# Weight signs by a parametric ReLU, 128-row values, long weight rows and filling products from the start, in an attention and channel-mix kernel

## The chip, the cores and the metric

The kernel runs on one core of one Trainium2 chip. The core has five engines that work side by side, each through its own instructions in order: TensorE (PE in the profile, its weight loads PEld), VectorE (DVE), ScalarE (ACT), GpSimd (POOL) and SyncE (SP), which here issues every DMA. The metric is the device time of one execution in microseconds; lower is better.

## The reference

Two blocks follow each other: attention with a local window and block summaries, and a gated channel mix over the concatenated heads.

```python
# attention: B, H, S, D = 4, 8, 768, 64; block 32, window 16
k_sum = k.reshape(B, H, nb, block, D).max(axis=3)
v_sum = v.reshape(B, H, nb, block, D).mean(axis=3)
scores_l = scale * q @ k^T, masked to |i - j| < 16
scores_s = scale * q @ k_sum^T + log(block)
a = softmax(concatenate([scores_l, scores_s]))
attn = a @ concatenate([v, v_sum])
# channel mix: x = attn as (4, 768, 512); d_ff = 1024
x_prev = x shifted by one token
xk = mu_k * x + (1 - mu_k) * x_prev
xr = mu_r * x + (1 - mu_r) * x_prev
k = maximum(xk @ w_k, 0)
out = sigmoid(xr @ w_r) * ((k * k) @ w_v)
```

The weights arrive in double precision, everything else in single.

## The kernel before

**Tiling.** The tokens of each of the four batches are cut into two halves of 384 (hf 0 and 1), the heads into four pairs p. A *unit* is one pair of one half: its scores (L466, 24 passes into sc), mask and row minimum on VectorE (L477), exponentials with row sums on ScalarE (L481), inverse sums (L487, L488), normalisation on GpSimd (L493), transposes on TensorE (L500), their copy to SBUF (L504), the product with the values (L513, into av) and the copy of the result (vx, L524 or L526). Each score tile has 120 columns: 64 + 32 keys of the window and 24 block maxima, which VectorE makes of the keys (L381 to L393). The values stand in vx with 120 rows to match; the block means are a product with the small table pool_sb (L405), a copy, a selection (L425) and a copy into the 24 middle rows (L431).

**Mix, gate, experts.** L535 or L538 and L541 mix a half's result with its shifted self. For the very first half (batch 0, hf 0) gate and experts work in plain float32: L580 multiplies the mixes of pair p with w_r (12 products into three PSUM tiles), L558 takes the sigmoid of each tile into z, L601 is xk @ w_k (one j of eight, 128 columns of w_k), L608 and L610 are ReLU and square, L627 the product with w_v. For the seven other halves each operand is split into a high and a low part, and each product is three (L567 to L569 for the gate, L601 and L627 again for the experts).

**Weights.** They are sent as 64-bit words. A weight step loads 128 rows of 4096 bytes into one of three buffers st (L310; w_k comes as four runs of 1024 bytes in each row), then builds float32 of the two words: ScalarE (L318) or GpSimd (L321) scales the upper word, read as a float, into wc; VectorE shifts three bits out of the lower word into the single buffer we (L325), puts the sign of the upper word beside them (L328), and joins both (L332). There are 20 steps: four of w_r, eight of w_k and eight of w_v in turn. Later L349 or L350 (high part) and L352 (low part) split each.

**Order.** Nothing is issued as written. All operations are recorded with an expected length (table LENGTH), a due time and the buffers they take, and a planner (`schedule`) plays the engines through: at each step it takes for each engine the operation that can start first or is due first, and gives buffers in turn. An operation with two ways, like L318 and L321, goes to the engine that would end it first. Loads are played as one queue with a fixed time and so many bytes a nanosecond. The engines then run the instructions in the planned order, waiting where reality is later. Up to 150 filling products (`warm`, L680: identity by identity, once the identity has landed) may be placed where TensorE has nothing due, until the last of the float32 gate is planned.

Of the kernel before, what the change touches and what calls it, by code (L numbers as in the profile page):

```python
# [18 lines left out]
DM, DF = 512, 1024  # L19
# [24 lines left out]
    exp=380, pts=380, vm=160, mixa=520, cast=405, relu=525, square=530, sigmoid=500, wscale=570, wcast=530,  # L44
# [4 lines left out]
DMA_NS_PER_BYTE = 1 / 290.0  # L49
# [8 lines left out]
WARM = 150  # L58
COLD = 10000
# [39 lines left out]
class Plan:  # L99
# [36 lines left out]
    def schedule(self):  # L136
# [27 lines left out]
        spare = [o for o in self.ops if o.name == "warm"]  # L164
        while any(ready.values()):
            best = None
            for e, now in engines.items():
# [53 lines left out]
            if o.name == "gate32" and spare:  # L221

                for w in spare:
                    for x in w.bufs:
                        x.left -= 1
                        if not x.left:
                            free_slots[x.pool].append((start, x.place))
                spare = []
                ready["PE"] = [x for x in ready["PE"] if x[0].name != "warm"]
            if o.name == "warm":  # L230
                spare.remove(o)
# [8 lines left out]
def tile_kernel(ctx: ExitStack, tc: tile.TileContext, q, k, vT, v, mask, ident, pool, sel, mu, w_k, w_v, w_r, out):  # L240
# [36 lines left out]
    MASK, IDENT, MU, OM, POOLM, SEL = [((x, 0),) for x in ("mask", "ident", "mu", "om", "pool", "sel")]  # L277
# [23 lines left out]
    def weight(name, i, src, last, due=None):  # L301
        st, we, wc = buf("st"), buf("we"), buf("wc")
        wf = w_f[name, i] = buf("wc") if last else buf("w", F32, False)
        shape = src.shape
        whole = [(wc, 0)]

        def load():
            s = src.bitcast(U32)
            d = st.t.rearrange("p (c a) -> p c a", c=shape[1]) if len(shape) == 3 else st.t
            nc.sync.dma_start(out=d, in_=s)  # L310

        def words():
            w = st.t.rearrange("p (a b) -> p a b", b=2)
            return w[:, :, 1], w[:, :, 0]


        def scale_act():
            nc.scalar.activation(wc.t.bitcast(F32), words()[0].bitcast(F32), AF.Copy, scale=2.0**-112)  # L318
# [256 lines left out]
    def gate_parts(x, z):  # L575
# [7 lines left out]
        for t in range(NTT):  # L583
            sigmoid(ps[t], z[t])
# [218 lines left out]
```

## Time and profile before

| | |
|---|---|
| Time, median of three runs (lowest to highest) | 474.1 us (472.27 to 476.43) |
| The profiled execution's own time | 475.29 us |
| Its span, first to last instruction | 473.5 us |
| TensorE busy | 447.6 us (95%) |
| ScalarE busy | 292.6 us (62%) |
| VectorE busy | 267.0 us (56%) |
| GpSimd busy | 112.5 us (24%) |
| Mean granted TensorE clock | 0.993 of full speed |
| Moved by DMA | 51.16 MB, mean 108 GB/s |

Busy time is time in which an engine's instruction ran; for TensorE the ends of pipelined products are modelled. Times in the trace count from the first instruction. A row of the timeline or of the chain gives the start, the length, engine, line and tiles; "x24" is the number of instructions merged in it, and for TensorE one float32 product is two instructions (passes). What stands in brackets is the time the engine was idle before and what ended it. "issue" is time in which the profile shows nothing to wait for.

### The profile page before, as it was taken

To read this page: it belongs to the slowest core of one execution; us is meant where nothing else is said; L and a number is where in the kernel's file an instruction comes from. 1 tells how busy PE (TensorE), PEld (TensorE's weight loads), DVE (VectorE), ACT (ScalarE), POOL (GpSimd) and SP (SyncE) were. 2 spreads that over 40 slices of the span, in tenths; PEclk is the share of its full clock that TensorE was granted. 3 is DMA by queue.
4 is the path that set the end of the run, shared out by engine and by line. 5 is a ranking of instruction groups with operands and counts; after the bars stand their busy time and mean duration, and the time that the engine had idled before them with its cause. 6 is when DMAs were issued, how large, how long until landed. Compare 5 with 4: busy or idle time off the path is not lost.

```text
span 473.5 us, 9475 instructions
## 1 busy us (share of the span) xinstructions
PE 447.6 (95%) x3438; PEld 357.9 (76%) x3438; DVE 267.0 (56%) x865; ACT 292.6 (62%) x815; POOL 112.5 (24%) x236
## 2 busy tenths in 40 slices
PE   2798799989899999999999999999999999999996
PEld 2664455546688888997778888997778889888995
DVE  3599789989453566527554565529354554222223
ACT  3578987878785756418886756428886655231311
POOL 0453470734133201302442201304242201000000
PEclk9999889999999999999999999999999999999999
DMA  7995368986110209807200219707100010001001
GB/s 245 257 261 158 105 207 262 289 263 148 51 59 12 68 1 304 211 0 228 60 8 9 78 37 301 212 1 219 35 9 9 12 43 26 1 0 68 0 1 66
DMA packets 27013, 51.16 MB, mean 108 GB/s; under 512 B 2903, under 2 KB 14807, under 8 KB 26967
## 3 DMA queue, kind: packets, MB, share of 16 engines
q1 hardware_dynamic: 26967, 50.56, 36.7%
q8 instruction: 27, 0.44, 0.4%
q14 instruction: 19, 0.16, 0.1%
HBM read 42.49 MB, written 6.29 MB: 103 GB/s over the span
## 4 chain that ended last, share of the span: by engine, by line
PE 67%; ACT 12%; DVE 8%; DMA 8%; issue 2%; POOL 1%; SPq 1%; ACTq 0%; POOLq 0%; DVEq 0%
PE mm L627 23%; PE mm L601 22%; ACT y L481 5%; PE pt L500 4%; PE av L513 4%; DMA kt<-in_k 3%; PE mm L567 3%; PE mm L569 3%; PE mm L568 3%; PE sc L466 2%; DMA pool_sb<-in_pool 2%; PE mm L580 2%; ACT L481 2%; DMA st<-in_w_k 1%; POOL y L493 1%
## 5 line engine op out<-in xcount | busy, mean ns | idle before, releaser
L601 PE MATMUL mm<-xs,w 128*128 128x384 f32 x736 | 152.1, 355 | 0.6 <-DVE w L332 0.6
L601 PEld LDWEIGHTS mm<-xs,w 128*128 128x128 f32 x736 | 131.3, 190 | 13.9 <-issue 3.7
L493 POOL TENSOR_SCALAR y<-y,rc 128x120 f32<-128x120 f32 x192 | 93.9, 507 | 156.1 <-DVE rc L488 131.6
L627 PE MATMUL mm<-w,kh 128*128 128x512 f32 x336 | 91.9, 402 | 0.0
L608 ACT ACTIVATE r<-mm 128x384 f32<-128x384 f32 x64 | 31.2, 488 | 93.9 <-PE mm L601 93.8
L481 ACT ACTIVATE y<-y,mn 128x120 f32<-128x120 f32 x192 | 73.5, 386 | 10.7 <-DVE mn L477 10.4
L627 PEld LDWEIGHTS mm<-w,kh 128*128 128x128 f32 x336 | 60.7, 188 | 11.1 <-DVE kl L616 0.2
L614 DVE CAST kh<-r 128x384 fp32r<-128x384 f32 x44 | 15.9, 362 | 74.9 <-ACT r L610 74.8
L477 DVE CUSTOM_DVE_ANT_0 y<-sc,mask_sb 128x120 f32<-128x120 f32 x192 | 42.5, 277 | 22.9 <-PE sc L466 19.6
L627 PE MATMUL mm<-w,kl 128*128 128x512 f32 x168 | 52.4, 407 | 0.1
L549 DVE TENSOR_TENSOR xs<-xa,xs 128x384 fp32r<-128x384 f32 x56 | 30.4, 558 | 23.6 <-ACT xs L547 23.2
L500 PE MATMUL pt<-ident_sb,y 128*120 128x128 f32 x192 | 33.9, 285 | 6.4 <-POOL y L493 6.0
L504 ACT COPY pts<-pt 120x384 f32<-120x384 f32 x64 | 30.3, 473 | 15.6 <-PE pt L500 15.4
L466 PE MATMUL sc<-kt,qt 64*64 64x120 f32 x768 | 30.4, 289 | 8.6 <-DMA pool_sb<-in_pool 6.8
L500 PEld LDWEIGHTS pt<-ident_sb,y 128*120 128x120 f32 x192 | 22.8, 139 | 19.0 <-POOL y L493 9.6
L481 ACT ACTIVATION_READ_ACCUMULATOR y<-y,mn 128x1 f32 x192 | 36.3, 189 | 0.0
L541 DVE SCALAR_TENSOR_TENSOR xa<-vx,mu_sb,xa 128x384 f32<-128x384 f32 x56 | 33.8, 630 | 2.7 <-ACT xa L535 1.8
L627 PEld LDWEIGHTS mm<-w,kl 128*128 128x128 f32 x168 | 30.0, 188 | 6.5 <-DVE kl L616 0.5
L466 PEld LDWEIGHTS sc<-kt,qt 64*64 64x64 f32 x768 | 22.2, 143 | 16.7 <-DVE kt L393 6.8
L567 PE MATMUL mm<-w,xs 128*128 128x512 f32 x84 | 33.6, 400 | 1.1 <-ACT r L608 0.8
L610 ACT ACTIVATE r<-r 128x384 f32<-128x384 f32 x64 | 33.6, 525 | 1.2
L616 DVE TENSOR_TENSOR kl<-r,kh 128x384 fp32r<-128x384 f32 x56 | 31.7, 566 | 4.3 <-ACT kh L615 1.3
(64 smaller groups left out, 548.1 us busy)
## 6 DMA issues: line engine op xcount, KB each, us to landing
vx<-in_v SPq DMA_DIRECT2D x32, 360.0 KB
kt<-in_k SPq DMA_DIRECT2D x15, 544.0 KB
qt<-in_q SPq DMA_DIRECT2D x32, 192.0 KB
out<-z SPq DMA_DIRECT2D x24, 256.0 KB
st<-in_vT SPq DMA_DIRECT2D x12, 384.0 KB
st<-in_w_k SPq DMA_DIRECT2D x8, 512.0 KB
st<-in_w_v SPq DMA_DIRECT2D x8, 512.0 KB
st<-in_w_r SPq DMA_DIRECT2D x4, 512.0 KB
```

The lines of the kernel that those rows point to most:

```text
L466: nc.tensor.matmul(sc[h].t[cs, i, 0:NK], qt.t[hs, n * QW:(n + 1) * QW], kt.t[hs, w * KB:w * KB + NK], start=True, stop=True,)
L477: op("DVE", "mask", None, lambda h=h, i=i, var=var: nc.vector.tensor_tensor_reduce(out=y[h].t[:, i, :], in0=sc[h].t[:, i, 0:NK], in1=mask_ ...
L481: op("ACT", "exp", None, lambda h=h, i=i: nc.scalar.activation(y[h].t[:, i, :], y[h].t[:, i, :], AF.Exp, bias=mn[h].t[:, i:i + 1], scale=-1.0,
L493: op("POOL", "norm", None, lambda h=h, i=i: nc.gpsimd.tensor_scalar(out=y[h].t[:, i, :], in0=y[h].t[:, i, :], scalar1=rc.t[:, NSL * h + i: ...
L500: nc.tensor.transpose(out=pt[h].t[0:NK, i * P:(i + 1) * P], in_=y[h].t[:, i, :], identity=ident_sb)
L541: op("DVE", "mixd", None, lambda: nc.vector.scalar_tensor_tensor(out=xa.t, in0=xt.t[:, 1 + lo:1 + lo + HT], scalar=mu_sb[:, which, p:p + 1 ...
L567: nc.tensor.matmul(ps.t, xh.t[:, ts], h, start=(p == 0), stop=False)
L601: nc.tensor.matmul(ps.t[:, 0:HT], w.t[:, p * P:(p + 1) * P], (x[p] if single else x[p][s]).t, start=(n == 0), stop=(n == len(terms) * NPAI ...
L608: op("ACT", "relu", None, lambda: nc.scalar.activation(r.t, ps.t[:, 0:HT], AF.Relu), reads=[(ps, 0)], writes=[(r, 0)])
L610: op("ACT", "square", None, lambda: nc.scalar.activation(r.t, r.t, AF.Square), reads=[(r, 0)], writes=[(r, 0)])
L616: op("DVE", "sub", None, lambda: nc.vector.tensor_tensor(out=kl.t, in0=r.t, in1=kh.t.bitcast(F32), op=ALU.subtract), reads=[(r, 0), (kh, 0 ...
L627: nc.tensor.matmul(acc[t].t, a.t[:, t * P:(t + 1) * P], v.bitcast(F32) if single else v, start=start, stop=stop)
```

## The change

1. **Weight step.** The scaling on ScalarE becomes a parametric ReLU whose slope for negative inputs, -2^32, leaves the sign where the following shift puts it. VectorE's step for the sign (L328) and GpSimd's way (L321) go. So st is read last by L307 (ScalarE) and L310 (VectorE), lines of the new kernel.
2. **Loads.** w_k is laid out beforehand so that each row of a step is one run of 4096 bytes; the values are padded from 120 to 128 rows (384 KB a load in place of 360).
3. **Filling products** multiply a tile of zeros that GpSimd sets at the start, write the unused end of the transposes' PSUM tile (so they hold no mm tile), and may be placed up to 110 us of the plan wherever TensorE would else be idle for over 0.3 us.
4. **Sigmoids** of the first half are one operation of the plan, so they stand side by side.
5. The planner is told other numbers: 330 bytes a nanosecond for loads in place of 290, and 4.0 us for the three sigmoids.

```diff
-DMA_NS_PER_BYTE = 1 / 290.0
+DMA_NS_PER_BYTE = 1 / 330.0
-WARM = 150
-COLD = 10000
+WARM = 260
+WARM_END = 110000
+GAP = 300
+COLD = 5000
...
+                if e == "PE" and now > WARM_END:
+                    ready[e] = [x for x in ready[e] if x[0].name != "warm"]
                 for o, at in ready[e]:
+                    if o.name == "warm":
+                        fill = max(now, at), o
+                        continue
...
+                if fill and (pick is None or pick[2] > fill[0] + GAP):
+                    pick = None, fill[1], fill[0]
...
-        def scale_act():
-            nc.scalar.activation(wc.t.bitcast(F32), words()[0].bitcast(F32), AF.Copy, scale=2.0**-112)
...
-        def sign():
-            nc.vector.scalar_tensor_tensor(
-                out=we.t, in0=words()[0], scalar=0x80000000, in1=we.t, op0=ALU.bitwise_and, op1=ALU.bitwise_or)
...
+        op("ACT", "wscale", None, lambda: nc.scalar.activation(
+            wc.t.bitcast(F32), words(1).bitcast(F32), AF.Prelu, scale=2.0**-112, alpha=-2.0**32),
+           reads=[(st, 0)], writes=[(wc, 0)])
...
-                out=windows(vw[hf]), in_=v[b, p, hf]),
-               writes=[(vw[hf], "a"), (vw[hf], "b")], size=NK * HW * 512)
+                out=vw[hf].t[:, 0:S], in_=v[b, p, hf]),
+               writes=[(vw[hf], "a"), (vw[hf], "b")], size=P * HW * 512)
...
-        for t in range(NTT):
-            sigmoid(ps[t], z[t])
+        def sigmoids():
+            for t in range(NTT):
+                nc.scalar.activation(z[t].t, ps[t].t, AF.Sigmoid)
+        op("ACT", "sigmoid3", None, sigmoids, reads=[(a, 0) for a in ps], writes=[(a, 0) for a in z])
...
-    spare = buf("mm", F32, False)
+    op("POOL", "tiny", -1.0e6, lambda: nc.gpsimd.memset(zero_sb, 0.0), writes=ZERO)
+    spare = pools["pt"][0][:, 512 - P:512]
     for _ in range(WARM):
         op("PE", "warm", 1.0e8, lambda: nc.tensor.matmul(
-            spare.t[:, 0:P], ident_sb, ident_sb, start=True, stop=True), reads=IDENT, writes=[(spare, 0)])
+            spare, zero_sb, zero_sb, start=True, stop=True), reads=ZERO)
...
-        "w_k": words(inputs["moe_w_k"]),
+        "w_k": words(np.asarray(inputs["moe_w_k"]).reshape(NCK, P, NCV, P).transpose(2, 1, 0, 3), NCV),
```

The planned order on TensorE at the program's start, before (sc: scores of the first and second unit; then pooling and the first transposes; rows left out repeat their neighbours):

```order
L466 MATMUL sc_128<-kt_61,qt_64 64x120 x2
L466 MATMUL sc_129<-kt_61,qt_64 64x120 x2
...
L466 MATMUL sc_128<-kt_62,qt_65 64x120 x2
L466 MATMUL sc_129<-kt_62,qt_65 64x120 x2
...
L405 MATMUL mm_132<-vx_68,pool_sb 32x128 x2
...
L500 MATMUL pt_130<-ident_sb,y_91 120x128 x3
```

and after, with the same names:

```order
L660 MATMUL pt_130<-zero_sb 128x128 x13
L441 MATMUL sc_128<-kt_61,qt_64 64x120 x2
L441 MATMUL sc_129<-kt_61,qt_64 64x120 x2
...
L660 MATMUL pt_130<-zero_sb 128x128 x13
L441 MATMUL sc_128<-kt_62,qt_65 64x120 x2
...
L660 MATMUL pt_130<-zero_sb 128x128 x5
L380 MATMUL mm_132<-vx_68,pool_sb 32x128 x2
...
L475 MATMUL pt_130<-ident_sb,y_91 120x128 x3
```

31 filling products stand before the first pooling where none stood; between there and the last values of the first half are 12 more where 15 were.

TensorE again, from the end of the first half's last values (L513, L488 after) to the transposes of the next unit, before:

```order
L513 MATMUL av_131<-pts_106,vx_77 64x64
L466 MATMUL sc_128<-kt_61,qt_64 64x120 x2
...
L580 MATMUL mm_135<-w_0_524,xs_0_561 128x512
L580 MATMUL mm_133<-w_0_524,xs_0_561 128x512
L580 MATMUL mm_134<-w_0_524,xs_0_561 128x512
L601 MATMUL mm_132<-xs_0_565,w_0_563 128x384
...
L466 MATMUL sc_128<-kt_62,qt_65 64x120 x2
...
L500 MATMUL pt_130<-ident_sb,y_91 120x128 x3
```

and after (xs_0_527 is the third pair's mix, xs_0_578 the fourth's):

```order
L488 MATMUL av_131<-pts_106,vx_77 64x64
L555 MATMUL mm_135<-w_0_513,xs_0_527 128x512
L555 MATMUL mm_132<-w_0_513,xs_0_527 128x512
L441 MATMUL sc_128<-kt_61,qt_64 64x120 x2
...
L660 MATMUL pt_130<-zero_sb 128x128
L555 MATMUL mm_133<-w_0_546,xs_0_578 128x512
...
L441 MATMUL sc_128<-kt_62,qt_65 64x120 x2
...
L660 MATMUL pt_130<-zero_sb 128x128 x5
L475 MATMUL pt_130<-ident_sb,y_91 120x128 x3
L660 MATMUL pt_130<-zero_sb 128x128 x2
```

Two gate products of the third pair now follow the last values, and eight filling products have come in.

ScalarE in the same place, before (wc: a weight step; z: a sigmoid; y: exponentials of the next unit; r: ReLU and square of the first expert):

```order
L318 ACTIVATE wc_126<-st_122 128x512
L349 CAST w_0_581<-w_0_563 128x512
L558 ACT_TABLE_LOAD
L558 ACTIVATE z_108<-mm_135 128x512
L481 ACT_TABLE_LOAD
L481 ACTIVATE y_91,sm_100<-y_91,mn_95 128x120 x3
L481 ACTIVATE y_92,sm_100<-y_92,mn_96 128x120 x3
L558 ACT_TABLE_LOAD
L558 ACTIVATE z_109<-mm_133 128x512
L558 ACTIVATE z_110<-mm_134 128x512
L318 ACTIVATE wc_127<-st_123 128x512
L608 ACTIVATE r_116<-mm_132 128x384
```

and after:

```order
L307 ACTIVATE wc_126<-st_122 128x512
L456 ACTIVATE y_91,sm_100<-y_91,mn_95 128x120 x3
L456 ACTIVATE y_92,sm_100<-y_92,mn_96 128x120 x3
L561 ACT_TABLE_LOAD
L561 ACTIVATE z_108<-mm_133 128x512
L561 ACTIVATE z_109<-mm_135 128x512
L561 ACTIVATE z_110<-mm_132 128x512
L587 ACTIVATE r_116<-mm_134 128x384
L479 COPY pts_107<-pt_130 120x384
L589 ACTIVATE r_116<-r_116 128x384
L307 ACTIVATE wc_127<-st_123 128x512
```

The exponentials of the next unit now stand ahead of the sigmoids, and the first sigmoid's own pair of table loads is gone.

More of the change, by code (lines that the diff above doesn't have):

```diff
@@ L163, in schedule @@
                 released(o)
-        spare = [o for o in self.ops if o.name == "warm"]
         while any(ready.values()):
@@ L220, in schedule @@
             order.append(o)
[L221 to L231, printed above, removed]
             for s in o.succ:
@@ L276, in tile_kernel @@
     sel_sb = const.tile([P, NS], F32, name="sel_sb")
-    MASK, IDENT, MU, OM, POOLM, SEL = [((x, 0),) for x in ("mask", "ident", "mu", "om", "pool", "sel")]
+    zero_sb = const.tile([P, P], F32, name="zero_sb")
+    MASK, IDENT, MU, OM, POOLM, SEL, ZERO = [((x, 0),) for x in ("mask", "ident", "mu", "om", "pool", "sel", "zero")]
     op("SP", "load", None, lambda: nc.sync.dma_start(out=mask_sb, in_=mask), writes=MASK, size=P * 3 * NK * 4)
@@ L331, in join @@
-        def join():
-            nc.vector.scalar_tensor_tensor(
-                out=wf.t.bitcast(U32), in0=wc.t, scalar=3, in1=we.t, op0=ALU.logical_shift_left, op1=ALU.bitwise_or)
-        op("SP", "load", due, load, writes=[(st, 0)], size=P * 4096)
-        op("ACT", "wscale", None, scale_act, reads=[(st, 0)], writes=whole, other=("POOL", "wscale_p", scale_pool))
-        op("DVE", "wbits", None, low, reads=[(st, 0)], writes=[(we, 0)])
-        op("DVE", "wor", None, sign, reads=[(st, 0), (we, 0)], writes=[(we, 0)])
@@ L339, in weight, with words @@
-        op("DVE", "wor", None, join, reads=[(we, 0), *whole], writes=[(wf, 0)])
+        def words(n):
+            return st.t.rearrange("p (a b) -> p a b", b=2)[:, :, n]
+        op("SP", "load", due, lambda: nc.sync.dma_start(out=st.t, in_=src.bitcast(U32)), writes=[(st, 0)], size=P * 4096)
+        op("ACT", "wscale", None, lambda: nc.scalar.activation(
+            wc.t.bitcast(F32), words(1).bitcast(F32), AF.Prelu, scale=2.0**-112, alpha=-2.0**32),
+           reads=[(st, 0)], writes=[(wc, 0)])
@@ L672, in tile_kernel @@
     for i in range(NCK):
-        weight("wr", i, w_r[i * P:(i + 1) * P, :], False)
+        weight("wr", i, w_r[i], False)
     for j in range(NCV):
-        weight("wk", j, w_k[:, j * P:(j + 1) * P].rearrange("(c p) n -> p c n", p=P), False)
-        weight("wv", j, w_v[j * P:(j + 1) * P, :], j == NCV - 1)
-    spare = buf("mm", F32, False)
+        weight("wk", j, w_k[j], False)
+        weight("wv", j, w_v[j], j == NCV - 1)
+    op("POOL", "tiny", -1.0e6, lambda: nc.gpsimd.memset(zero_sb, 0.0), writes=ZERO)
+    spare = pools["pt"][0][:, 512 - P:512]
     for _ in range(WARM):
-        op("PE", "warm", 1.0e8, lambda: nc.tensor.matmul(
-            spare.t[:, 0:P], ident_sb, ident_sb, start=True, stop=True), reads=IDENT, writes=[(spare, 0)])
+        op("PE", "warm", 1.0e8, lambda: nc.tensor.matmul(spare, zero_sb, zero_sb, start=True, stop=True), reads=ZERO)
     sets, gates = [], []
```

35 lines of the change are left out of this document (13 added, 22 removed).

## The prediction

> **What bounds the kernel now.** I read the windows first, cut where the work changes, then the chain of waits of the first 64 us, then the timeline of TensorE where the windows show holes, then the groups by line. Rows of the windows give the stretch, its length, and busy time (with the count of instructions) of PE, PEld, DVE, ACT and POOL, then the granted clock, the DMA share and GB/s:
>
> ```profile
> 16.00:43.00 27.00, 27.00 (x320) 17.89 (x320) 22.21 (x63) 18.38 (x55) 14.55 (x23) 1.00 0.82 220
> 43.00:62.00 19.00, 14.10 (x85) 7.75 (x78) 13.84 (x53) 18.82 (x51) 5.31 (x9) 0.82 0.47 145
> 62.00:109.00 47.00, 44.50 (x311) 24.79 (x309) 44.63 (x128) 37.13 (x107) 21.32 (x37) 1.00 0.87 258
> 109.00:126.00 17.00, 14.66 (x126) 11.01 (x127) 12.14 (x40) 14.10 (x37) 7.25 (x14) 1.00 0.31 78
> 126.00:474.00 348.00, 342.37 (x2539) 292.93 (x2537) 167.19 (x545) 198.46 (x546) 61.45 (x140) 1.00 0.24 72
> ```
>
> The last row settles where a gain can come from: from 126 us to the end TensorE is busy for 342.4 of 348.0 us. The order of its products is the same there in both programs but for a few transposes near the start, so that stretch keeps its length, and the change is worth what it lets that stretch start earlier. Before it, TensorE has no hole from 16 to 43 us, but part of what it does there is filler and part runs slowly; from 43 to 62 us it stands still for 4.9 us and is granted 0.82 of its clock; from 62 to 126 us it stands still for 2.5 + 2.3 = 4.8 us. VectorE is busy for 44.6 of the 47 us after 62 us, so it is next.
>
> The chain of waits up to 64 us, start, length and what (the first line shares the 64 us out):
>
> ```profile
> by line: DMA pool_sb<-in_pool 13.3%; PE mm L580 13.0%; ACT y L481 9.0%; PE mm L680 7.1%; PE pt L500 6.3%; PE mm L405 6.1%; PE av L513 5.3%; ACT L558 4.0%; ACT L481 4.0%; ACT wc L318 3.9%; PE sc L466 3.4%; ACT xs L535 3.4%; SPq L371 3.1%; is
> 6.07 8.51 DMA pool_sb<-in_pool
> 14.63 1.51 PE mm L405 x24
> 16.13 0.83 PE pt L500 x3
> 16.96 1.41 PE sc L466 x24
> 18.37 0.55 PE mm L425 x2
> 18.92 0.83 PE pt L500 x3
> 19.75 1.70 PE mm L680 x10
> 22.30 0.47 PE pt L500 x3
> 22.77 0.45 PE mm L680 x4
> 23.22 0.79 PE mm L405 x24
> 24.93 0.33 PE mm L425 x2
> 25.90 0.78 PE sc L466 x24
> ```
>
> The small table pool_sb takes 8.5 us to land, because it stands in the queue behind keys and values; the first pooling products (L405) wait for it. Until about 21 us the same products take almost twice what they take later (L405 1.51 against 0.79): TensorE is cold, whatever the clock column says there. And 7.1% of the 64 us, 4.5 us, are filling products (L680), of which ten passes took 0.17 us each cold and later ones 0.11.
>
> **The change, part by part.** *128-row values.* The windows from 6 us on show what the loads get:
>
> ```profile
> 6.00:9.00 3.00, 1.48 (x24) 1.13 (x24) 0.97 (x3) 0.00 (x0) 0.00 (x0) 1.00 0.99 371
> 9.00:14.00 5.00, 2.07 (x24) 1.38 (x24) 4.13 (x32) 3.24 (x17) 0.98 (x3) 1.00 1.06 245
> 14.00:32.00 18.00, 17.37 (x225) 13.06 (x226) 11.98 (x47) 12.29 (x47) 8.40 (x19) 1.00 1.01 257
> ```
>
> The engines are as full in all three, yet they move 371 GB/s while keys, queries and masks (128 rows each) are under way, and 245 to 257 once values of 120 rows are among them. I take it that the 120 rows fall badly on the engines and slow all that runs beside them, and that loads of 128 rows get the 371. Bounds: nothing, down to 7% worse (128 rows instead of 120 at 245 GB/s), and 371. Two value loads stand ahead of pool_sb. [...] Pooling starts **1.6 us** sooner. [...]
>
> *4096-byte weight rows* for w_k: 8 loads. From 43 to 62 us, where the first of them run, the share of the DMA engines is 0.47, so the load is not what ends last; nothing.
>
> *Early filling products.* 31 of them (62 passes) now stand before the first pooling, of which 13 before the first scores and 13 before the second. They wait for a zeroed tile, one MEMSET on a GpSimd with nothing to do then. Cold, 13 take 26 x 0.17 = 4.4 us; the first scores start at 6.85 us:
>
> ```profile
> 6.85 1.48 PE L466 MATMUL sc<-kt,qt 64*64 64x120 f32 x24 [6.85 <-DMA pool_sb<-in_pool]
> 10.11 2.07 PE L466 MATMUL sc<-kt,qt 64*64 64x120 f32 x24 [1.79 <-DVE mn L477]
> ```
>
> so the first 13 fit. The second 13 fit into 7.7 to 10.6 us if warm (26 x 0.11 = 2.9); if cold, they would hold the second scores back by 2 us, and this is the bound on the bad side. With TensorE warm, the pooling, two transposes, scores and selection of the chain above go from 1.51 + 2 x 0.83 + 1.41 + 0.55 to 0.79 + 2 x 0.47 + 0.78 + 0.33: **2.3 us**. Of the 4.5 us of fillers, 12 (24 passes, 2.7 us) remain between the first pooling and the last values of the first half: **1.8 us**, if nothing else is late there. What is late next is the softmax of the last pair, whose transposes wait for GpSimd.
>
> *The stretch around the sigmoids.* TensorE's timeline, with idle time before a row and its releaser in brackets:
>
> ```profile
> 44.77 2.84 PE L580 MATMUL mm<-w,xs 128*128 128x512 f32 x6 [1.47 <-DVE xs L541]
> 47.45 2.74 PE L601 MATMUL mm<-xs,w 128*128 128x384 f32 x8
> 50.12 0.84 PE L466 MATMUL sc<-kt,qt 64*64 64x120 f32 x24
> 53.95 0.33 PE L500 MATMUL pt<-ident_sb,y 128*120 128x128 f32 x1 [2.98 <-POOL y L493]
> 54.72 0.81 PE L500 MATMUL pt<-ident_sb,y 128*120 128x128 f32 x2 [0.44 <-POOL y L493]
> 55.45 1.71 PE L466 MATMUL sc<-kt,qt 64*64 64x120 f32 x24
> 57.10 5.17 PE L601 MATMUL mm<-xs,w 128*128 128x384 f32 x8
> ```
>
> and ScalarE's part of the chain there:
>
> ```profile
> 46.83 1.28 ACT L558
> 48.12 0.60 ACT z L558
> 48.74 1.28 ACT L481
> 56.33 1.28 ACT L481
> ```
>
> Two gate products of the third pair (2.84 / 3 = 0.95 us each) now stand behind the last values and cover the wait for the last pair's mix: **1.5 us**. The first sigmoid with a table load on each side, 1.28 + 0.60 + 1.28 = 3.2 us, stood before the exponentials of the next unit; now these come first. Their transposes, at 53.95 us before, are ready 3.2 us sooner, at 50.8, when TensorE has just done the next scores at 51.0. Eight fillers (1.8 us) stay in the order there, so of the 3.4 us idle **1.6 us** go. With no hole of this size the clock should not fall: L601 5.17 against 2.74 and L466 1.71 against 0.84, **3.3 us**. [...]
>
> *The weight step.*
>
> ```profile
> L328 DVE SCALAR_TENSOR_TENSOR we<-st,we 128x512 uint32<-128x512 uint32 x20 | 14.8, 738 | 0.1
> L318 ACT ACTIVATE wc<-st 128x512 f32<-128x512 f32 x15 | 10.2, 678 | 2.9 <-DMA st<-in_w_k 2.1 <-DMA st<-in_w_v 0.7
> L349 ACT CAST w<-w 128x512 fp32r<-128x512 f32 x16 | 9.8, 613 | 2.9 <-DVE w L332 2.7
> SPq L310 <- DVE we L328: 51.9, 17, 6.2
> ```
>
> VectorE loses L328, 20 x 0.738 = 14.8 us, which hides behind TensorE today and keeps it from becoming the bound when TensorE comes earlier. SP's queue loses a wait of the same name (17 weight loads waited for a buffer that L328 was last to read; queries and keys stand behind them). A Prelu is not in the trace; I price it as the same ACTIVATE with Copy, 0.678 us, from below by the cast (0.613), from above by two passes (1.36). All 20 now lie on ScalarE, where 15 did. From the last values to the first gate of the second half ScalarE had
>
> ```profile
> 43.00:112.00 69.00, 61.26 (x407) 34.72 (x399) 61.46 (x191) 58.95 (x166) 26.63 (x45) 0.95 0.76 226
> ```
>
> 58.95 us. By the two orders it loses there two table loads (2.6) and six casts that go to GpSimd (3.7), and gains three weight steps (2.0) and one copy (0.5): 55.2 us. TensorE needs 61.3 - 3.3 + 1.8 = 59.8 us there. ScalarE is then 92% full, in order, so I charge **1.5 us** of new waits, and let the 4.8 us idle between 62 and 126 us stand.
>
> Sum: 1.6 + 2.3 + 1.8 + 1.5 + 1.6 + 3.3 - 1.5 = 10.6 us. The profiled span was 473.5 us, so the new span is 462.9; that run's own time was 1.8 above its span, the median of the three runs 0.6. Forecast: 474.1 - 10.6 = 463.5 us.
>
> **The rivals.**
> - *The value loads are no faster.* [...] Then the start (1.6) and the denser middle (1.8) are lost and some other wait comes with them: 474.1 - 7.0 = 467. [...] Against it: 371 and 245 GB/s at the same share.
> - *ScalarE becomes the bound* between 43 and 112 us: 92% full leaves 4.6 us, and squares, evacuations and exponentials each have someone waiting. With 5 us of new waits in place of 1.5: 467. For it: it was busy for 18.8 of 19 us from 43 to 62. Against it: part of that was table loads.
> - *The clock falls all the same* after the fillers: 3.3 us less, 467.
> - *Slower: Prelu takes more than two passes.* 15 of them lie in the stretch where ScalarE has 4.6 us to spare. At d us above Copy, 15 d - 4.6 us are lost; against 10.6 + 1.5 gained it decides from d = 1.1, and at d = 1.4 (2.1 us each, three passes) the time is 474.1 - 12.1 + 16.4 = 478. Against it: casts, copies and sigmoids of 512 columns all lie at 0.6 to 0.7 us.
> - *Better still:* the middle runs without a filler's worth of waiting and half of the later 4.8 us goes: 458.
>
> **How the numbers follow.** Forecast (460 to 466.5) 0.50; value loads no faster 0.16; ScalarE the bound 0.15; clock falls 0.08; better 0.07; slower 0.04. The range 457 to 469 leaves out Prelu's bad end and the tails of the 467 cases. One per cent, 4.7 us, is about what a measurement of this kernel can tell from no change: faster means under 469.4. That holds for the forecast, the better case and most of the three 467 cases: 0.84; within 1%: 0.12; slower 0.04.
>
> **What would show it.** Pooling starting near 13 us at 0.8 us; GB/s of some 370 from 9 us on; the last values of the first half ending near 36 us (42.5 before); no clock under 0.95 from 30 to 60 us; a Prelu near 0.68 us; ScalarE not named before long TensorE waits; the stretch of even products starting some 10 us sooner and ending as long after. Wrong it would be if TensorE, in order, stood behind a new wait for weights or ScalarE after 50 us, or if the fillers held back ready work.

## The result and the profile after

| | before | after |
|---|---|---|
| Median of four runs each on one chip (lowest to highest) | 473.74 us (472.27 to 476.43) | 461.48 us (460.97 to 462.56) |
| Span of the profiled execution | 473.5 us | 460.8 us |
| Mean granted TensorE clock | 0.993 | 0.999 |

The ratio is 0.9736, with a 95% interval from 0.9706 to 0.9766: some 12.5 us less, 2 us more than the 10.6 us of the forecast. In the profiled executions the gain falls to three stretches (the marks are the end of the first half's last values, before 42.53 us and after 36.43, and the start of the second half's first gate product, before 109.34 and after 95.37):

| | forecast | measured |
|---|---|---|
| up to the last values | 1.6 + 2.3 + 1.8 = 5.7 | 6.1 |
| from there to the gate | 1.5 + 1.6 + 3.3 - 1.5 = 4.9 | 7.9 |
| from the gate to the end | 0 | -1.3 |
| sum | 10.6 | 12.7 |

The sum is close, but the first two rows do not cut the same work. Before, 18 of the first half's 24 gate passes stand ahead of its last values, after the change 14: the two products of the third pair went behind them. These four passes take 1.9 us. Like for like the first stretch gained 4.2 us and the second 9.8. What brought this about is the larger part of what follows.

The windows of the changed kernel, cut at the same kinds of work as those of before (stretch, its length, busy time and count of PE, PEld, DVE, ACT and POOL, then granted clock, DMA share, GB/s):

```profile
6.00:9.00 3.00, 2.66 (x41) 2.34 (x40) 1.17 (x5) 0.00 (x0) 0.00 (x0) 1.00 1.01 352
9.00:14.00 5.00, 5.00 (x81) 4.23 (x84) 4.23 (x32) 4.06 (x22) 1.93 (x6) 1.00 1.03 383
14.00:26.00 12.00, 10.86 (x183) 8.40 (x180) 10.16 (x42) 10.89 (x42) 6.45 (x14) 1.00 0.95 367
50.00:95.30 45.30, 45.30 (x334) 25.36 (x333) 41.26 (x129) 41.49 (x125) 26.18 (x39) 1.00 0.79 268
95.30:115.00 19.70, 16.03 (x137) 12.35 (x136) 8.30 (x34) 13.34 (x35) 5.49 (x15) 1.00 0.33 111
115.00:460.80 345.80, 340.71 (x2532) 291.71 (x2529) 166.82 (x546) 197.92 (x546) 60.01 (x139) 1.00 0.22 73
```

From 9 us on the loads get 383 and 367 GB/s where they got 245 (9 to 14 us) and 257 (14 to 32 us), and from 50 to 95.3 us TensorE does not stand still at all. The last stretch is as even as it was: 5.1 us idle in 345.8, against 5.6 in 348 before. VectorE has 41.26 us of work in the 45.3, so 4.0 to spare; this number is needed below.

TensorE's timeline of the changed kernel, where the holes and the halved clock stood before (start, length, engine, line, tiles), and the two long waits left behind them:

```profile
36.36 1.98 PE L555 MATMUL mm<-w,xs 128*128 128x512 f32 x4
38.28 0.85 PE L441 MATMUL sc<-kt,qt 64*64 64x120 f32 x24
39.05 0.49 PE L660 MATMUL pt<-zero_sb 128*128 128x128 f32 x2
39.38 2.74 PE L555 MATMUL mm<-w,xs 128*128 128x512 f32 x6
41.95 2.74 PE L580 MATMUL mm<-xs,w 128*128 128x384 f32 x8
44.63 0.84 PE L441 MATMUL sc<-kt,qt 64*64 64x120 f32 x24
45.40 1.38 PE L660 MATMUL pt<-zero_sb 128*128 128x128 f32 x10
46.62 0.49 PE L475 MATMUL pt<-ident_sb,y 128*120 128x128 f32 x3
...
101.65 0.50 PE L542 MATMUL mm<-w,xs 128*128 128x512 f32 x1 [1.98 <-ACT z L533]
...
112.39 0.51 PE L475 MATMUL pt<-ident_sb,y 128*120 128x128 f32 x3 [1.69 <-POOL y L468]
```

No row from 36 to 47 us has a bracket, so nothing is waited for there; before, 1.47, 2.98 and 0.44 us were, and the next eight passes of the experts took 5.17 us at half the clock (granted 0.50 from 55 to 61 us). The group of the new weight step (count, busy time in us, mean ns of one, idle time before):

```profile
L307 ACT ACTIVATE wc<-st 128x512 f32<-128x512 f32 x20 | 13.1, 677 | 0.1
```

A parametric ReLU takes 677 ns, a Copy took 678: nothing on top.

### The profile page after: what moved, and what is told of

Read it like the earlier page. It is cut to its first block, busy times and chain, and to the rows that moved or that the text cites. A ratio compares the mean times of both kernels' runs of the same rounds, so it can differ in the third digit from the quotient of the medians.

```text
span 460.8 us, 9597 instructions
## 1 busy us (share of the span) xinstructions
PE 449.6 (98%) x3510; PEld 363.2 (79%) x3510; DVE 254.7 (55%) x846; ACT 288.1 (63%) x811; POOL 112.3 (24%) x238
## 4 chain that ended last, share of the span: by engine, by line
PE 88%; ACT 7%; POOL 2%; SPq 1%; DVE 1%; issue 1%; DMA 0%; POOLq 0%; ACTq 0%
PE mm L606 29%; PE mm L580 28%; PE pt L475 5%; PE av L488 5%; PE sc L441 4%; PE mm L542 4%; PE mm L543 4%; PE mm L544 4%; ACT y L456 3%; PE mm L555 2%; PE pt L660 2%; POOL y L468 2%; ACT L456 1%; ACT pts L479 1%; PE mm L380 1%
## 5 line engine op out<-in xcount | busy, mean ns | idle before, releaser
L580 PE MATMUL mm<-xs,w 128*128 128x384 f32 x736 | 149.8, 352 | 0.0
L580 PEld LDWEIGHTS mm<-xs,w 128*128 128x128 f32 x736 | 130.4, 188 | 12.5 <-issue 1.4
L468 POOL TENSOR_SCALAR y<-y,rc 128x120 f32<-128x120 f32 x192 | 91.2, 493 | 167.5 <-DVE rc L463 138.7
L606 PEld LDWEIGHTS mm<-w,kh 128*128 128x128 f32 x336 | 60.7, 188 | 11.2 <-issue 0.2
L475 PE MATMUL pt<-ident_sb,y 128*120 128x128 f32 x192 | 32.7, 279 | 3.0 <-POOL y L468 2.5
L542 PE MATMUL mm<-w,xs 128*128 128x512 f32 x84 | 33.6, 399 | 2.0 <-ACT z L533 2.0
L488 PEld LDWEIGHTS av<-pts,vx 120*64 120x64 f32 x768 | 25.2, 137 | 11.4 <-issue 10.0
L544 PE MATMUL mm<-w,xs 128*128 128x512 f32 x84 | 32.8, 391 | 0.0
```

The costliest lines, as they stand in the source:

```text
L468: op("POOL", "norm", None, lambda h=h, i=i: nc.gpsimd.tensor_scalar(out=y[h].t[:, i, :], in0=y[h].t[:, i, :], scalar1=rc.t[:, NSL * h + i: ...
L475: nc.tensor.transpose(out=pt[h].t[0:NK, i * P:(i + 1) * P], in_=y[h].t[:, i, :], identity=ident_sb)
L488: nc.tensor.matmul(av.t[hs, w * QW:(w + 1) * QW], windows(vw)[:, w, hs], pts[h].t[:, i, c * QW:(c + 1) * QW], start=True, stop=True,)
L542: nc.tensor.matmul(ps.t, xh.t[:, ts], h, start=(p == 0), stop=False)
L544: nc.tensor.matmul(ps.t, xl.t[:, ts], h, start=False, stop=(p == NPAIR - 1))
L580: nc.tensor.matmul(ps.t[:, 0:HT], w.t[:, p * P:(p + 1) * P], (x[p] if single else x[p][s]).t, start=(n == 0), stop=(n == len(terms) * NPAI ...
```

## The experiments

Twelve kernels ran. Two undo the loads, two the weight step, one the sigmoids, one the weight rows, two the fillers; three do one or two parts alone on the kernel before; one tries to beat both. Ratios are against the kernel before on the same chip (its medians there were 473.7 to 474.4 us); differences in us are differences of ratios times 474 unless said otherwise. The last columns are read from TensorE's timeline of each profile: the start of the first pooling, the end of the first half's last values, the start of the second half's first gate product, and the span. These marks compare fully only between kernels of one order: the kernels made from the one before have the four gate passes ahead of the last values, and before_prelu and before_prelu_v128 have one more product with the values and three more transposes, some 1.3 us, ahead of the gate.

| kernel | median us | ratio (95%) | pooling | last values | gate | span |
|---|---|---|---|---|---|---|
| before | 474.1 | 1 | 14.63 | 42.53 | 109.34 | 473.5 |
| before_v128 | 471.05 | 0.9919 (0.9888 to 0.9950) | 12.55 | 39.52 | 105.67 | 469.5 |
| before_prelu | 465.81 | 0.9844 (0.9818 to 0.9869) | 14.54 | 42.09 | 103.53 | 465.2 |
| before_prelu_v128 | 464.53 | 0.9806 (0.9782 to 0.9831) | 12.38 | 39.74 | 101.17 | 462.8 |
| after | 461.48 | 0.9736 (0.9706 to 0.9766) | 12.57 | 36.43 | 95.37 | 460.8 |
| v120 | 466.04 | 0.9813 (0.9777 to 0.9849) | 13.97 | 40.68 | 99.61 | 464.2 |
| v112_16 | 466.07 | 0.9821 (0.9783 to 0.9859) | 14.15 | 38.18 | 97.11 | 464.6 |
| sign_dve | 467.82 | 0.9859 (0.9822 to 0.9895) | 12.80 | 37.12 | 106.44 | 467.0 |
| sign_blind | 471.11 | 0.9950 (0.9928 to 0.9971) | 12.50 | 36.44 | 103.50 | 472.1 |
| sig_apart | 462.33 | 0.9739 (0.9699 to 0.9779) | 12.54 | 36.40 | 97.10 | 460.7 |
| late_fill | 462.90 | 0.9756 (0.9721 to 0.9791) | 12.20 | 37.89 | 96.82 | 461.1 |
| no_fill | 461.86 | 0.9733 (0.9695 to 0.9770) | 12.31 | 36.44 | 94.67 | 459.1 |
| wk4 | 461.29 | 0.9724 (0.9689 to 0.9758) | 12.65 | 36.51 | 95.45 | 459.7 |
| no_fill_e2 | 459.81 | 0.9712 (0.9688 to 0.9736) | 12.25 | 36.69 | 97.19 | 458.0 |

### The value loads

v120, on the changed kernel:

```diff
-                out=vw[hf].t[:, 0:S], in_=v[b, p, hf]),
+                out=vw[hf].t[0:NK, 0:S], in_=v[b, p, hf, 0:NK]),
```

> The changed kernel, but each value load moves only the 120 rows that are read, as before the change; every engine's order is the same, row for row. Theory (120 rows fall badly on the DMA engines and slow all loads beside them): GB/s from 9 to 14 us falls from 383 to 245 to 260, the first pooling starts near 14.2 us instead of 12.6, the last values of the first half end near 40 us instead of 36.4, and the two terms of the forecast that rest on the loads come back: 461.5 + 1.6 + 1.8 = 465 us. [...]

The windows of v120, columns as above:

```profile
9.00:14.00 5.00, 3.54 (x50) 3.07 (x50) 4.20 (x30) 3.55 (x19) 1.42 (x5) 1.00 1.05 274
14.00:26.00 12.00, 9.77 (x158) 7.47 (x158) 6.65 (x30) 8.76 (x31) 6.50 (x15) 1.00 1.02 260
```

The engines are as busy as in the changed kernel (1.05 and 1.02), and move 274 and 260 GB/s in place of 383 and 367. Pooling is 1.4 us later, the last values 4.3, the span 3.4. The theory holds, and the prediction's first rival, that the value loads are no faster, falls.

v112_16, on the changed kernel, asks whether the bytes of a value load count or its rows:

```diff
-            op("SP", "load", None, lambda hf=hf: nc.sync.dma_start(
-                out=vw[hf].t[:, 0:S], in_=v[b, p, hf]),
+            def load_values(hf=hf):
+                for lo, hi in ((0, 112), (112, P)):
+                    nc.sync.dma_start(out=vw[hf].t[lo:hi, 0:S], in_=v[b, p, hf, lo:hi])
+            op("SP", "load", None, load_values,
```

> The changed kernel, but each value load of 128 rows is cut into one of 112 rows and one of 16, with the same bytes. [...]

Its windows:

```profile
9.00:14.00 5.00, 3.46 (x47) 2.99 (x45) 3.91 (x27) 3.14 (x17) 1.27 (x4) 1.00 1.00 224
14.00:26.00 12.00, 10.71 (x186) 8.44 (x187) 8.39 (x39) 10.06 (x39) 7.24 (x16) 1.00 1.04 303
```

The bytes are all those of the changed kernel; yet they run at 224 and 303 GB/s, where the changed kernel has 383 and 367. Of the three shapes tried, the one of all 128 rows alone is fast. That the time is v120's is chance: up to the last values v112_16 loses 1.8 us and v120 4.3, and v112_16 loses the rest behind the gate, where its clock falls. The number of requests has a part as well: an issue of a value load occupies SyncE for 0.33 to 1.03 us in the changed kernel (median 0.43), and the small table, issued at 5.79 us in the changed kernel, is issued at 7.46 here. But it does not explain the rate. The single packets of 3072 bytes in the traces, of the same size in all shapes, take 121 ns (median, 9 to 14 us) in the changed kernel and in before_v128 below, 201 in the kernel before, 185 in v120 and 208 in v112_16. Why a packet takes longer in these shapes, no run separates.

before_v128 does this part alone, on the kernel before; every engine's order stays (the values are laid out with 128 rows beforehand, as in the changed kernel):

```diff
-                out=windows(vw[hf]), in_=v[b, p, hf]),
+                out=vw[hf].t[:, 0:S], in_=v[b, p, hf]),
...
```

> The kernel before, with only its value loads changed to 128 rows; every engine's order is the same, row for row. Theory (the loads are the gain of the start and of the middle): GB/s from 9 to 14 us rises from 245 to about 380, the first pooling starts at 13 instead of 14.6 us, and the time falls by the two terms, 3.4 us, or by the 4.6 us that the changed kernel lost with 120 rows: 469.6 to 470.8 against 474.2 us. Rival (the rest of that order, with its fillers, its hole around the sigmoids and the fallen clock, waits for something else and eats the gain): 473 to 474 us, with the landing early and the last values of the first half as late as before, 42.5 us.

Pooling 2.1 us sooner, the last values 3.0, the gate 3.7, the median 3.3 (471.05, a little above the theory's 469.6 to 470.8). TensorE's timeline of before_v128 shows what the loads do not mend:

```profile
41.77 2.84 PE L580 MATMUL mm<-w,xs 128*128 128x512 f32 x6 [1.47 <-DVE xs L541]
...
50.93 0.47 PE L500 MATMUL pt<-ident_sb,y 128*120 128x128 f32 x1 [2.96 <-POOL y L493]
...
52.43 1.71 PE L466 MATMUL sc<-kt,qt 64*64 64x120 f32 x24
54.08 4.62 PE L601 MATMUL mm<-xs,w 128*128 128x384 f32 x8
```

The same 1.47 and 2.96 us, the same products at half the clock (granted 0.50 from 51 to 57 us), 3 us sooner. The loads are worth 3.8 us alone (1 - 0.9919) and 3.7 us on top of the rest (0.9813 - 0.9736).

### The weight step

sign_dve, on the changed kernel:

```diff
-            wc.t.bitcast(F32), words(1).bitcast(F32), AF.Prelu, scale=2.0**-112, alpha=-2.0**32),
-           reads=[(st, 0)], writes=[(wc, 0)])
+            wc.t.bitcast(F32), words(1).bitcast(F32), AF.Copy, scale=2.0**-112),
+           reads=[(st, 0)], writes=[(wc, 0)], other=("POOL", "wscale_p", lambda: nc.gpsimd.tensor_scalar(
+               out=wc.t.bitcast(F32), in0=words(1).bitcast(F32), scalar1=2.0**-112, scalar2=1.0, op0=ALU.mult, op1=ALU.mult)))
...
+        op("DVE", "wor", None, lambda: nc.vector.scalar_tensor_tensor(
+            out=we.t, in0=words(1), scalar=0x80000000, in1=we.t, op0=ALU.bitwise_and, op1=ALU.bitwise_or),
+           reads=[(st, 0), (we, 0)], writes=[(we, 0)])
```

> The changed kernel with the weight step of before: a Copy on ScalarE or GpSimd, and the sign taken over on VectorE in a step of its own (20 x 0.74 us); the planner knows it and orders anew. From 50 to 95.3 us VectorE is busy for 41.3 of 45.3 us in the changed kernel; some 12 of the 20 steps lie there, 8.9 us. Theory (VectorE becomes the bound once TensorE comes early): 50.2 us of work in 45.3, so some 5 us later, 466 us. Rival (the 14.8 us hide behind TensorE as they did before the change, and ScalarE is relieved of up to five steps): 461 to 462 us.

A window of sign_dve:

```profile
62.00:85.00 23.00, 22.49 (x181) 13.14 (x179) 22.83 (x77) 19.55 (x63) 11.90 (x20) 1.00 0.77 265
```

VectorE has no time left (22.83 of 23 us here, 43.61 of 45.3 from 50 to 95.3), and the kernel is 5.8 us slower than the changed one. But the planner, told of the step, had also put 28 filling passes around the sigmoids where the changed kernel has 14, so sign_blind keeps the changed kernel's order and only has the extra instruction:

```diff
+        def low():
+            nc.vector.tensor_scalar(out=we.t, in0=words(0), scalar1=29, scalar2=None, op0=ALU.logical_shift_right)
+            nc.vector.scalar_tensor_tensor(
+                out=we.t, in0=words(1), scalar=0x80000000, in1=we.t, op0=ALU.bitwise_and, op1=ALU.bitwise_or)
...
+        op("DVE", "wbits", None, low, reads=[(st, 0)], writes=[(we, 0)])
```

(and the Copy in place of the parametric ReLU, as above.)

> The changed kernel with a Copy in place of the parametric ReLU and the sign step put back on VectorE behind each first weight step (20 x 0.74 us), the planner not told: every engine's order is that of the changed kernel. It leaves out what the planner made of the sign step in the earlier run. Theory (VectorE is the bound from 50 to 95 us with it): 8.9 us of work go into a stretch where VectorE has 4.0 to spare, so some 5 us more, 466.5 us, with TensorE waiting for VectorE. Rival (the planner's other order, with 28 filling passes around the sigmoids, made the loss): under 463 us.

10.1 us more than the changed kernel, and twice what the theory had. First a window of sign_blind, then rows of its TensorE timeline:

```profile
50.00:95.30 45.30, 42.47 (x302) 23.59 (x300) 42.62 (x125) 36.12 (x110) 25.09 (x37) 1.00 0.68 231
```

```profile
40.75 2.84 PE L559 MATMUL mm<-w,xs 128*128 128x512 f32 x6 [1.21 <-DVE xs L520]
...
49.05 1.00 PE L479 MATMUL pt<-ident_sb,y 128*120 128x128 f32 x3 [0.78 <-POOL y L472]
...
64.12 0.52 PE L479 MATMUL pt<-ident_sb,y 128*120 128x128 f32 x3 [0.83 <-ACT pts L483]
...
96.68 0.28 PE L399 MATMUL pt<-ident_sb,vs 128*24 128x128 f32 x1 [2.51 <-DVE vs L396]
...
110.42 0.79 PE L546 MATMUL mm<-w,xs 128*128 128x512 f32 x1 [2.59 <-ACT z L537]
111.02 0.63 PE L547 MATMUL mm<-w,xs 128*128 128x512 f32 x1
```

The last values end at 36.44 us as in the changed kernel, and then the wait ahead of the gate products is back, 1.21 us of the 1.47, put down to VectorE, though the two gate products that were meant to cover it still stand in front of it. Further waits that the changed kernel does not have are charged to GpSimd (0.78) and ScalarE (0.83), though only VectorE was given more to do. The gate of the second half comes 8.1 us late, the wait for its sigmoid grows from 1.98 to 2.59 us, and behind that the clock falls (granted 0.50 from 110 to 116 us): products of 0.63 us, 0.40 in the changed kernel. (This execution was the longest of its twelve, 473.9 us; most others had a mean clock of 0.995 or 0.996 in place of 0.992, so about half of that fall.) The rival, the planner's order, falls: without it the loss is larger, not smaller.

before_prelu is the reverse, this part alone on the kernel before (the planner knows it):

```diff
-            nc.scalar.activation(wc.t.bitcast(F32), words()[0].bitcast(F32), AF.Copy, scale=2.0**-112)
+            nc.scalar.activation(wc.t.bitcast(F32), words()[0].bitcast(F32), AF.Prelu, scale=2.0**-112, alpha=-2.0**32)
...
-        op("ACT", "wscale", None, scale_act, reads=[(st, 0)], writes=whole, other=("POOL", "wscale_p", scale_pool))
+        op("ACT", "wscale", None, scale_act, reads=[(st, 0)], writes=whole)
...
-        op("DVE", "wor", None, sign, reads=[(st, 0), (we, 0)], writes=[(we, 0)])
```

> The kernel before, with only the weight step of after: a parametric ReLU on ScalarE, no sign step on VectorE, no way over GpSimd; the planner knows it and orders anew. Theory (the 14.8 us of VectorE already cost before the change: the 1.47 us ahead of the gate products are put down to VectorE, and what follows is late with it): some 6 us less, as much as the changed kernel loses without it: 468 us. Rival (they hide as long as the loads are slow, and only bind once TensorE comes early): 472.5 to 474.5 us.

465.81 us: 7.4 us less (6.2 to 8.6 by the interval), with the loads as slow as ever (pooling at 14.54 us). The rival said that nothing is to be had as long as the loads are slow; it falls. Rows of TensorE's timeline of before_prelu:

```profile
43.91 0.42 PE L465 MATMUL sc<-kt,qt 64*64 64x120 f32 x4 [1.05 <-DVE mn L476]
...
47.97 5.32 PE L600 MATMUL mm<-xs,w 128*128 128x384 f32 x16
53.12 0.49 PE L499 MATMUL pt<-ident_sb,y 128*120 128x128 f32 x3
55.67 1.98 PE L626 MATMUL mm<-w,r 128*128 128x512 f32 x4 [2.05 <-ACT r L609]
```

16 passes of the experts take 5.32 us here, where 8 took 5.17 before: the clock does not fall. The longest hole there is 2.05 us in place of 2.98. The last values end only 0.4 us sooner than before, but the gate of the second half 5.8 us, and of that 5.8 the clock is 3.3 us by the prediction's rows.

The order is a new one, though, and ScalarE shows what it changed:

```profile
45.12 0.39 ACT L480 ACTIVATE y<-y,mn 128x120 f32<-128x120 f32 x1
...
47.50 1.28 ACT L557 ACT_TABLE_LOAD   x1
48.80 1.08 ACT L557 ACTIVATE z<-mm 128x512 f32<-128x512 f32 x2
```

The exponentials of the next unit stand ahead of the sigmoids, as in the changed kernel, though the sigmoids are still three operations here: once the sign step is gone the planner puts them so. The 7.4 us are therefore those of the step and of the order that goes with it; no run takes the step away with the order of before.

before_prelu_v128 has both parts, by the two diffs above, and nothing else of the change:

> The kernel before with the weight step of after and value loads of 128 rows, and nothing else of the change: its fillers, its three sigmoids apart, its planner's numbers stay. Theory (these two parts are the gain; fillers, sigmoids and weight rows add nothing that the runs without them could show): the time is within 1.5 us of the changed kernel, 461.5 to 463 us, and the clock does not fall. Rival (the other parts carry the some 2.5 to 3 us that the two leave, the loss to the fallen clock among them): 464.5 to 466 us, with half the clock for some us after the second half's first scores.

464.53 us, so the rival has the time right, but not the reason: the clock is 1.00 throughout. The two parts give 9.2 us together, less than 3.8 + 7.4 = 11.2, and leave 3.3 us to the rest of the change. The last values of the first half end at 39.74 us here and at 36.43 in the changed kernel, but 1.9 us of this difference are the four gate passes that the changed kernel does later. From there to the gate TensorE stands still for 3.8 us here (the waits of before_prelu again), and not at all in the changed kernel.

### Sigmoids, weight rows, fillers

sig_apart, on the changed kernel:

```diff
-        op("ACT", "sigmoid3", None, sigmoids, reads=[(a, 0) for a in ps], writes=[(a, 0) for a in z])
+        for t in range(NTT):
+            sigmoid(ps[t], z[t])
```

> The changed kernel with the three sigmoids of the first half as three operations, which the planner puts apart, as before the change, with a table load on each side. Theory: the exponentials of the next unit wait for one sigmoid and two table loads again (3.2 us), TensorE gets its idle time back: 1.6 us, and 3.3 more if the clock falls with it: 463 to 466.4 us. Rival (other work now covers it): 461.5 us, with the clock at 1.00 throughout.

TensorE's timeline of sig_apart:

```profile
47.79 2.82 PE L577 MATMUL mm<-xs,w 128*128 128x384 f32 x8 [2.35 <-DVE w L312]
...
54.45 0.52 PE L475 MATMUL pt<-ident_sb,y 128*120 128x128 f32 x3 [0.93 <-ACT pts L479]
```

Holes come back, 2.35 and 0.93 us, but no fillers stand there any more, the clock holds, and span and ratio are those of the changed kernel within the error (0.9739 and 0.9736). The theory's loss is there up to the gate, which starts 1.7 us later than in the changed kernel, but it is made good behind it, where the wait of 1.98 us is missing. Sigmoids in one go are worth nothing in the time that these runs can tell.

wk4 reads w_k in four pieces of 1024 bytes a row again (the load and the layout beforehand follow):

```diff
-        weight("wk", j, w_k[j], False)
+        weight("wk", j, w_k[:, j * P:(j + 1) * P].rearrange("(c p) n -> p c n", p=P), False)
...
```

> The changed kernel with w_k read as before, each row of 4096 bytes in four pieces of 1024; every engine's order is the same. Theory (they run in a stretch where the DMA engines have room): 461.5 us, no difference. Rival (small packets are slower and the loads beside them are late): some 1 to 2 us more, 463 us.

461.29 us: no difference, as the prediction had it. The pieces are slower for their size, as the rival says (in the trace of before, from 30 to 60 us, a packet of 1024 bytes takes 46 ns and one of 4096 takes 159, medians), but the time does not show it.

late_fill keeps the fillers back until the identity has landed, no_fill has none:

```diff
-            spare, zero_sb, zero_sb, start=True, stop=True), reads=ZERO)
+            spare, zero_sb, zero_sb, start=True, stop=True), reads=[*ZERO, *IDENT])
```

```diff
-WARM = 260
+WARM = 0
```

> The changed kernel without the 62 filling passes ahead of the first pooling (fillers may start only when the identity table has landed); 20 of the other fillers stay in their places. Theory (TensorE is cold without them): the first scores take about 1.5 us again, pooling 1.5 instead of 0.79, and the start is 2.3 us longer: 463.8 us. Rival (the ten passes right before the pooling, 1.3 us, hold it back, and a cold start is made good by starting sooner): pooling starts before 12.6 us and the time is 461 to 462.5 us.

> The changed kernel with no filling product at all. Theory: 2.3 us for the cold start as in the run without the early ones, and the holes that the fillers filled stay idle, some 2 us around the sigmoids, less than the 2.98 and 0.44 us after which the clock fell before the change: no clock under 0.95, 463.8 us. Rival (the later fillers are what holds the clock): half the clock for 6 to 7 us after 47 us, 3.3 us more, 467 us.

Both theory and rival of no_fill are wrong: it is as fast as the changed kernel. late_fill lies between its theory and its rival; by the ratios it is 0.9 us slower than the changed kernel, which the intervals do not tell from nothing. The start of the three, from TensorE's timelines, with GpSimd's copy (POOL); the changed kernel first:

```profile
14.94 0.55 PE L475 MATMUL pt<-ident_sb,y 128*120 128x128 f32 x3
15.33 0.83 PE L660 MATMUL pt<-zero_sb 128*128 128x128 f32 x6
15.64 0.82 POOL L406 COPY vx<-vm 24x768 f32<-24x768 f32 x1 [1.50 <-issue]
16.73 0.94 PE L660 MATMUL pt<-zero_sb 128*128 128x128 f32 x6 [0.57 <-ACT pts L479]
17.59 0.92 PE L488 MATMUL av<-pts,vx 120*64 120x64 f32 x24
```

no_fill:

```profile
12.31 1.51 PE L380 MATMUL mm<-vx,pool_sb 120*32 120x128 f32 x24 [0.64 <-DMA pool_sb<-in_pool]
...
16.72 0.82 POOL L406 COPY vx<-vm 24x768 f32<-24x768 f32 x1 [2.82 <-issue]
17.59 0.98 PE L488 MATMUL av<-pts,vx 120*64 120x64 f32 x24 [0.81 <-POOL vx L406]
```

late_fill:

```profile
18.18 0.94 PE L660 MATMUL pt<-zero_sb 128*128 128x128 f32 x6 [0.57 <-ACT pts L479]
19.05 0.92 PE L488 MATMUL av<-pts,vx 120*64 120x64 f32 x24
```

Without fillers TensorE is cold (1.51 for the pooling), and still the first values start at 17.59 us, as in the changed kernel: they wait for GpSimd's copy of the block means. In the changed kernel the products ahead are warm and that copy is 1.1 us earlier (15.64 against 16.72), and then six filling passes hold the values up for 0.94 us. Cold and with those fillers, in late_fill, they start 1.46 us later. So with these fillers the warm start gains 1.5 us, and the fillers between take as much; a warm start without them was not run. Later it is the same: at 45.4 us ten filling passes stand ahead of transposes, and the next product of the experts starts at 47.40 us, against 46.68 without fillers. The clock of no_fill stays at 1.00 after the cold start.

### A version meant to beat both

no_fill_e2, without fillers and with the last product of w_v due earlier:

```diff
-            due = e2_due(b, hf, j)
+            due = e2_due(b, hf, j) if not single or j < NCV - 1 else E2LAST
```

(E2LAST = 92000; WARM = 0.)

> A version that could beat both: the changed kernel without fillers, and the last product of the first half's second weights due at 92 us instead of 101.6, so that it stands between the gate products of the second half, whose second tile waits 1.98 us for a sigmoid. Theory (that wait, and the 1.69 us behind it, are filled by 2.8 us of work that stood later): some 2 us less than without fillers, 459.5 us. Rival (the wait only moves to the next tile or to the next half): 461 to 462 us.

A window of it:

```profile
95.30:115.00 19.70, 19.09 (x162) 14.59 (x158) 10.58 (x49) 14.19 (x40) 5.70 (x15) 1.00 0.50 159
```

TensorE is busy for 19.09 of the 19.7 us there, 16.03 in the changed kernel; the waits of 1.98 and 1.69 us are gone. (Its gate starts later because more work stands ahead of it, one of the moved products among it.) 459.81 us: all six runs (459.34 to 460.46) lie below all four of the changed kernel. By the ratios the gain over it is 1.1 us, and their intervals overlap, so it is likely but not settled. no_fill shows that the fillers alone gave none of it that can be told.

## Why the prediction came out right, and where it was wrong

The time lies in the range and on the right side, and nearly every event that the prediction named is in the trace. That the sum came so near is in part luck. Like for like the stretch up to the last values gained 1.5 us less than forecast (4.2 for 5.7), the one from there to the gate 4.9 more (9.8 for 4.9), and 1.3 us came back behind it. One step of the reasoning failed, and it is the largest of the change.

- **The loads.** Right in cause, and in size at the start: 371 GB/s were foreseen, 383 measured; pooling 1.6 us sooner, measured 2.1. (The 1.6 rests on some 0.6 us from the last byte of the small table to its landing, which no run shows; the trace of before has 0.9, from 13.70 to 14.58 us. With 0.9, from 9.0 us to the last packet pass 4.7 us at 245 GB/s, 1.15 MB; with 0.05 MB of padding and at 371 GB/s this takes 3.2, so the term is 1.5.) The whole part is worth 3.7 us by taking it away and 3.8 by doing it alone. That the terms put on it, 1.6 and 1.8, come so near is luck: the 1.8 was worked out from fewer fillers, and before_v128 keeps all of its own. The first rival (no faster, 467 us) is refuted by v120, which loses 3.7 us with 120 rows.
- **The step that failed: VectorE's sign step "hides behind TensorE today".** It was costed at nothing; taking it away alone, with the order that the planner then finds, is worth 7.4 us on the kernel before. The other half of the sentence, that it would become the bound once TensorE comes earlier, is borne out: putting it back on the changed kernel costs 5.8 us, or 10.1 where the order stays. But it had no term in the sum, and without this part the change gives 6.7 us (sign_dve) in place of 12.5. The rows that spoke against "hides" were shown: VectorE busy for 44.6 of 47 us, and 1.47 us of TensorE's idle time put down to VectorE itself. With VectorE busy for 42.6 of 45.3 us, sign_blind waits in places where the changed kernel does not, and part of that is charged to others: 0.78 us to GpSimd and 0.83 to ScalarE.
- **Idle 1.47 covered (1.5), the stretch of the sigmoids (1.6), the clock (3.3).** All three came, 6.4 us together, but not by the edits named alone. For the 1.47 us both are needed: sign_blind has the two gate products in place and waits 1.21 us all the same; before_prelu has VectorE relieved, without the two products there, and waits 1.05 and 0.18; the changed kernel has both and does not wait. For the other two the mechanism was right and its cause was not: with the exponentials ahead of the sigmoids the hole shrinks and the clock holds, but the planner puts them there as soon as the sign step is gone (before_prelu), and with the sigmoids apart nothing is lost that can be measured in the time (sig_apart).
- **Warm TensorE (2.3) and the denser middle (1.8).** From the pooling to the last values these two promise 4.1 us; like for like 2.1 came (4.0 by the marks, less the 1.9 us of products moved), and not by the parts named. The products are as fast as was said, 0.79 and 0.47 in place of 1.51 and 0.83, and no_fill, which is cold and has no fillers at all, ends its last values at the same 36.44 us. The step took TensorE as what ends last at the start, where GpSimd's copy does, or fillers that stand in the way. That the remaining fillers cost time the prediction saw; that they cost what the early ones gain, it did not.
- **New waits on ScalarE (-1.5) and the idle time of later left as it was.** ScalarE is as full as foreseen (41.49 of 45.3 us, 92%), and between the last values and the gate TensorE does not wait for it; the 2.8 us that TensorE stood still between 62 us and the gate (0.57 and 1.48 put down to VectorE, 0.79 to ScalarE) went too. These two make 9.2 of the 9.8 us out of 4.9. Behind the gate 1.3 us come back: 3.7 us idle from 95.3 to 115, 2.3 in the same place before. The profiled execution is the longest of its four, however; in wk4, of the same order, the wait of 1.98 us is 0.80, and the stretch behind the gate is 364.3 us long, as before (364.2).
- **The rivals.** The loads were faster, ScalarE was not the bound, the clock did not fall, and Prelu took a Copy's time (677 ns against 678). Of the better case (458 us) the later idle time went up to the gate, but the time of 461.48 us is the forecast's own case.

What stays open: 3.3 us between before_prelu_v128 and the changed kernel. At the last values 1.4 us are left once the moved products are taken off, about what late_fill, as cold at the start, loses there (1.5). The rest may lie in the 3.8 us of waits between there and the gate. Taken out alone, neither sigmoids nor weight rows nor fillers account for it; the two gate products behind the last values and the planner's new numbers for loads were not tried alone. Nor was the order of before tried without its own fillers.

## What to carry to other kernels

An engine that is busy for 95% of a stretch (VectorE here, 44.6 of 47 us) can be on the path of whatever waits in that stretch, even where the timeline names another releaser: put a price on what is taken off it, by adding the work back with the order fixed (10.1 us here). Where a planner makes the order, a part taken alone changes the order too, so look at what moved before naming a cause, and compare marks only where the same work lies ahead of them. Load with all 128 rows, padded if need be: with 7% more bytes in the value loads, all loads together ran at a rate 40 to 60% higher here (383 and 391 GB/s against 274 and 245). A warm start and fillers paid nothing here that could be told (461.48 us with them, 461.86 without), since the first values started at 17.59 us in both, behind GpSimd's copy in the one and behind fillers in the other; a run with none at all is the cheapest test.

## What the runs showed of the hardware

**Rows of a load.** With the DMA engines full (share 1.00 to 1.06), 383 and 391 GB/s with value loads of 128 rows (after, before_v128, 9 to 14 us), 245 and 274 with 120 rows (before, v120), 224 with 112 and 16 (v112_16; 303 from 14 to 26 us, share 1.04).

**The clock.** It fell behind holes of 2.98 and 0.44 us with a product between (before; 2.96 and 0.30 in before_v128), of 2.52 us (v112_16) and of 2.59 us (sign_blind), and held after 2.51 us (sign_blind at 96.68), 2.35 (sig_apart) and 2.05 (before_prelu). Windows of one us of v112_16, whose hole ends at 103.94, the granted clock being the third number from the end:

```profile
104.00:105.00 1.00, 1.00 (x4) 0.79 (x5) 0.00 (x0) 1.00 (x3) 0.89 (x3) 0.95 0.05 20
105.00:106.00 1.00, 1.00 (x4) 0.77 (x3) 0.62 (x1) 0.15 (x1) 0.00 (x0) 0.50 0.00 0
...
108.00:109.00 1.00, 1.00 (x13) 0.65 (x15) 0.00 (x0) 0.41 (x1) 0.00 (x0) 0.84 0.00 0
```

and of sign_blind, whose hole ends at 110.42:

```profile
109.00:110.00 1.00, 0.00 (x0) 0.00 (x0) 0.41 (x3) 0.99 (x2) 0.79 (x3) 0.90 0.17 68
...
116.00:117.00 1.00, 1.00 (x21) 0.66 (x23) 0.00 (x0) 0.96 (x2) 0.00 (x0) 0.69 0.00 0
```

At half the clock a us counts 0.5, so it fell at 104.9 and came back at 108.3 in the one, 3.4 us, and fell at 109.8 and came back at 116.6 in the other, 6.8 us; once a us after the hole, once inside it. In before it was at half from 55.0 to 61.8 us by the same reading, 6.8 us. How long a hole is does not decide alone here, since 2.51 us held and 2.52 did not; what else does, no run separates.
